# Top-k attention and a squared-ReLU feed: blocks of scores handled two at a time

## The chip, the cores and the metric

The kernel runs on one core of a Trainium2 chip. Its metric is device time in microseconds: the median of three runs was 1082.91 us (1082.89 to 1084.41). Engines have in-order instruction streams of their own: TensorE (PE, with its weight loads shown as PEld), VectorE (DVE), ScalarE (ACT), GpSimd (POOL) and SyncE (SP, which issues all DMAs here). They meet only at semaphores.

## The reference

For 8 batches x 8 heads, q, k and v are 576 x 64 in fp32. The attention keeps, in each row of scores, those not below the row's 32nd largest:

```python
scores = scale * np.matmul(q, k.transpose(0, 1, 3, 2))        # 576 x 576 per head
kth = np.partition(scores, -32, axis=-1)[..., -32:-31]
scores = np.where(scores >= kth, scores, -1e9)
attn = softmax(scores)                                         # exp, sum + 1e-9
x = (attn @ v).transpose(0, 2, 1, 3).reshape(4608, 512)
out = np.maximum(x @ w_in, 0) ** 2 @ w_out                     # 512 -> 2048 -> 512
```

## The kernel before

**Blocks.** A block is 128 query rows by 576 keys. Two heads form a pair (`hp`; 4 pairs in a batch, 32 in all). Queries 0 to 511 of a pair give 4 groups `gi` of two blocks, one for each head; the last 64 queries of both heads share one more block, which goes with `gi` 3. So a pair has 9 blocks, the kernel 288.

**`load_pair`.** SP loads q, k and v of a pair; TensorE transposes q and k into `qk` (head dim on partitions), and GpSimd casts v into `vb` with a column of ones, whose product gives the softmax sums. The last 64 keys of both heads share one 128-row slab of `vb`, kept apart by two multiplications with `heads`.

**`top_k`.** TensorE makes a block's scores with queries on partitions (`scores`, `scores_last`), two halves of 288 keys in two PSUM banks; ScalarE copies them to `s`. The 32nd largest of 576 is found by folding: VectorE takes `m` = max of the two halves (288), and `pp` = max of the halves of `m` (144). GpSimd, through `whole`, makes the other parts by integer arithmetic on the bits: sums `t` of the halves, less the maximum, give the minima, which it writes into `f` behind 144 candidates of `pp`: `mid` (144 more) and `low` (288 more). VectorE then takes eight maxima at a time (`vec.max`) and replaces them (`match_replace`): once over `pp`, then over 144, 288 and 576 columns; each step adds eight, and the last gives `kth`. ScalarE makes `w` = relu(kth - s), which is 0 where a score is kept.

**`attend`.** It runs once for one or two groups `js` (with the 64-query block, where it belongs to them). TensorE computes the scores again, transposed, keys on partitions (`qkT`, fp32), adds `w` transposed and times a steep negative constant (`masked`, bf16 matmuls against `minus`), and ScalarE takes the exponential (`fE`; the last 64 keys apart, `fT4`). TensorE multiplies by `vb` (`fav`), ScalarE copies to `av`, VectorE takes reciprocals, GpSimd scales, TensorE transposes back, ScalarE copies into `xt`.

**`feed`.** When a chunk of `xt` is complete (576 rows; in the last batch 320, 128, 128), two bf16 matmuls with the squared ReLU between follow, and SP stores the rows.

**What sets the order.** Nothing above is emitted in program order. `Plan.op` records each operation with an engine, an assumed duration `dur`, a priority and its dependences; `Plan.schedule` simulates the five engines as a list scheduler and fixes the order of each engine's stream and all buffer slots (`Pool`); `Emitter` turns dependences into semaphore waits. Chip timing differs from the simulated one, but each engine keeps the planned order. Priorities are due times: `PER` us for one block, starting at `T0`. The planner treats VectorE and GpSimd as independent. A second plan with a slower method stands behind a branch and runs only if `verdict` finds ties that break the folding; it doesn't run with these inputs. All matmuls carry line 360 (helper `mm`), all transposes 363 (`tr`), GpSimd's integer operations 514 (`whole`).

Of the kernel before, what the change touches and what calls it, by code (L numbers as in the profile page):

```python
# [12 lines left out]
P = 128  # L13
# [7 lines left out]
class Pool:  # L21
# [16 lines left out]
    def find(self, width):  # L38
        if width == 1:
            if not self.free:  # L40
                return None
            if self.name == "psum":
                half = [s for s in self.free if (s ^ 1) not in self.free]
                s = half[0] if half else self.free[0]
            else:
                s = self.free[0]
            self.free.remove(s)
            return s
        for s in self.free:
            if s % width == 0 and all(s + i in self.free for i in range(width)):  # L50
# [26 lines left out]
class Op:  # L77
    __slots__ = ("eng", "dur", "prio", "fn", "deps", "tiles", "takes", "n", "users", "start", "end",
                 "idx", "sem", "val", "ndma", "seq", "vc", "waits", "wars", "later", "nbf")
# [5 lines left out]
class Plan:  # L85
# [3 lines left out]
    def op(self, eng, dur, prio, fn, r=(), w=(), u=(), hold=(), take=(), after=(), order=(), sem=None, ndma=0, nbf=0.0):  # L89
# [3 lines left out]
        o.eng, o.dur, o.prio, o.fn = eng, dur, prio, fn  # L93
        o.sem, o.ndma, o.seq, o.nbf = sem, ndma, len(self.ops), nbf
# [22 lines left out]
    def schedule(self, t0=0.0, latency=0.12, own=0.07):  # L117
# [22 lines left out]
        done = 0  # L140
        while events:
# [19 lines left out]
            for e in ENGS:  # L161
                if busy[e] > t + 1e-9:
                    continue
                skipped = []
                while ready[e]:
# [22 lines left out]
                    o.start = t  # L188
                    hold = o.dur if e != "sp" else 0.6 * o.ndma
                    o.end = t + o.dur + (hold if e == "sp" else 0)  # L190
                    busy[e] = t + hold
# [85 lines left out]
def bass_top_k_attn__then__act_relu_squared_kernel(  # L277
# [20 lines left out]
    def sb(name, shape, dt=FP32, n=None):  # L298
# [9 lines left out]
    kth = sb("kth", [P, 3, 4 * NPAIR + 8])  # L308
    c16 = sb("c16", [P, 3, 4 * NPAIR + 8])
    c24 = sb("c24", [P, 3, 4 * NPAIR + 8])  # L310
# [7 lines left out]

    sizes = {
        "rq": ([P, 5, 2, D], FP32, 2), "rk": ([P, 5, 2, D], FP32, 2), "rv": ([P, 9, D], FP32, 2),  # L320
        "qk": ([P, 2, S], FP32, 5), "vb": ([P, 10, D + 1], BF16, 5),
        "s": ([P, S], FP32, 8), "m": ([P, HALF], FP32, 4), "pp": ([P, QUART], FP32, 4),
        "t1": ([P, HALF], FP32, 2), "t2": ([P, QUART], FP32, 2), "f": ([P, S], FP32, 4),
        "a": ([P, 3, 8], FP32, 3), "sh": ([P, 3], FP32, 2), "w": ([P, S], BF16, 13),
        "p": ([P, 4, 2, 320], BF16, 3), "p4": ([P, 320], BF16, 3), "av": ([P, 5, D + 1], FP32, 2),
        "x": ([P, 5, D], BF16, 2), "xt": ([P, NCT, S], BF16, 3), "g": ([P, S], BF16, 16),
# [21 lines left out]

    def batch_order(b):
        if b < NB - 1:  # L350
            return ([(hp, g) for hp in range(NHP) for g in range(4)], {1: ([0, 1], False), 3: ([2, 3], True)},
                    [(0, S)])
        return ([(hp, g) for g in (2, 3, 0, 1) for hp in range(NHP)],
                {3: ([2, 3], True), 0: ([0], False), 1: ([1], False)}, [(256, 320), (0, 128), (128, 128)])

    PER = 3.2
    T0 = 12.0

# [3 lines left out]
    def tr(o, i, ident):  # L362
        return pe.matmul(o, i, ident, is_transpose=True, skip_group_check=True)  # L363

    def build(full, weights, pl):
        state = {"n": 0, "u": 0, "g": 0, "z": 0, "last": {}}
# [6 lines left out]
        def load_pair(b, hp, base):  # L373
# [12 lines left out]
            def loadv():  # L386
# [3 lines left out]
                res += [nc.sync.dma_start(r[64 * h:64 * h + 64, 8, :], v[b, 2 * hp + h, 512:576, :])  # L390
                        for h in range(2)]
# [4 lines left out]
            pl.op("sp", 2.3, base - 70, loadv, w=[rv], take=[rv], sem=slot_sem, ndma=4)  # L396
# [22 lines left out]
            pl.op("gp", .62, base + 5, lambda: gp.tensor_copy(at(vb)[:, 0:8, 0:D], at(rv)[:, 0:8, :]),  # L419
                  r=[rv], w=[vb], take=[vb])  # L420
            for h in range(2):
                pl.op("gp", .45, base + 5.1, lambda h=h: gp.tensor_scalar(
                    at(vb)[:, 8 + h, 0:D], at(rv)[:, 8, :], heads[:, h:h + 1], None, ALU.mult), r=[rv], w=[vb])
            return qk, vb

        def top_k(gi, qk, tg, dw):

            nb = 3 if gi == 3 else 2
            n0 = state["n"]
            state["n"] += nb  # L430
            ss = [Tile(psum, 2) for _ in range(nb)]
            st = [tile("s") for _ in range(nb)]

            def scores():
                x = at(qk)
                for half in range(2):
                    ks = HALF * half
                    for h in range(2):
                        ins = mm(bank(ss[h], half)[:, 0:HALF],
                                 x[64 * h:64 * h + 64, 0, 128 * gi:128 * gi + 128],  # L440
                                 x[64 * h:64 * h + 64, 1, ks:ks + HALF], True)
                return ins

            def scores_last():
                x = at(qk)
                for half in range(2):
                    for h in range(2):
                        ha = half ^ h
                        ins = mm(bank(ss[2], ha)[64 * h:64 * h + 64, 0:HALF],
                                 x[64 * h:64 * h + 64, 0, 512:576],  # L450
                                 x[64 * h:64 * h + 64, 1, HALF * ha:HALF * ha + HALF], True)
                return ins

            pl.op("pe", 1.2, tg - 30, scores, r=[qk], w=ss[:2], take=ss[:2] + st[:2])
            if nb == 3:
                pl.op("pe", 1.2, tg - 29, scores_last, r=[qk], w=[ss[2]], take=[ss[2], st[2]])
            for i in range(nb):
                pl.op("act", .64, tg - 28 + i, lambda i=i: act.copy(  # L458
                    at(st[i])[:, :].rearrange("p (a c) -> p a c", a=2),
                    ps32[:, ss[i].slot:ss[i].slot + 2, 0:HALF]), r=[ss[i]], w=[st[i]])  # L460

            a = tile("a")
            dk = [0]
            ix = [state["g"], state["g"], state["z"]]
            state["g"] += 1
            state["z"] += nb == 3

            def dve(dur, fn, **kw):
                dk[0] += 1
                return pl.op("dve", dur, tg + .34 * dk[0], fn, **kw)  # L470

            def eighth(t, i):

                return t[:, i, ix[i] + 7:(ix[i] - 1 if ix[i] else None):-1]
# [6 lines left out]
            ks = []  # L481
            if full:
                f = [tile("f") for _ in range(nb)]
                sh = tile("sh")
                prev = [[] for _ in range(nb)]
                for rnd in range(4):
                    src = st if rnd == 0 else f
                    for i in range(nb):
                        get = dict(r=[st[i]]) if rnd == 0 else dict(hold=[f[i]])
                        if rnd == 3:  # L490
                            ks.append(chain(kth, i, prev[i], .665, lambda i=i: vec.max(
                                eighth(kth, i), at(f[i])[:, :]), **get))
                            continue
                        prev[i] = [dve(.665, lambda i=i, src=src: vec.max(at(a)[:, i, :], at(src[i])[:, :]),
                                       after=prev[i], take=[a, sh] if rnd == 0 and i == 0 else [],
                                       w=[a] if rnd == 0 else [], **(
                                           get if rnd == 0 else dict(hold=[f[i], a])))]
                    if rnd == 3:
                        break
                    if rnd == 0:  # L500
                        prev[nb - 1].append(dve(.08, lambda: vec.tensor_scalar(
                            at(sh)[:, 0:nb], at(a)[:, 0:nb, 0], 0.0, None, ALU.max), r=[a], w=[sh]))
                        prev = [prev[nb - 1] + prev[i] for i in range(nb)]
                    for i in range(nb):
                        prev[i] = [dve(.725, lambda i=i, src=src: vec.match_replace(
                            at(f[i])[:, :], at(a)[:, i, :], at(src[i])[:, :], NEG), after=prev[i],
                            **(dict(r=[st[i]], w=[f[i]], hold=[a], take=[f[i]]) if rnd == 0
                               else dict(hold=[f[i], a])))]
            else:

                m, pp, t1, t2, f = ([tile(nm) for _ in range(nb)] for nm in ("m", "pp", "t1", "t2", "f"))

                def whole(dur, prio, i, op, o, x, y, **kw):
                    return pl.op("gp", dur, prio + .8 * i, lambda: gp.tensor_tensor(  # L514
                        o().bitcast(I32), x().bitcast(I32), y().bitcast(I32), op), **kw)

                low, mid = [], []
                for i in range(nb):
                    A, B = (lambda i=i: at(st[i])[:, 0:HALF]), (lambda i=i: at(st[i])[:, HALF:S])
                    M, L = (lambda i=i: at(m[i])[:, :]), (lambda i=i: at(t1[i])[:, :])  # L520
# [3 lines left out]
                for i in range(nb):  # L524
# [392 lines left out]
```

## Time and profile before

| | |
|---|---|
| median of 3 runs | 1082.91 us |
| profiled execution, its own time | 1080.87 us |
| its span | 1079.0 us |
| busy: DVE / PE / POOL / ACT | 980.8 / 918.1 / 906.7 / 765.9 us |
| mean granted TensorE clock | 0.954 of full speed |
| DMA, mean | 44 GB/s |

The span reaches from the first to the last instruction of one execution. A busy time is the time in which at least one instruction of that engine (or group) runs, so records that overlap by their ends count once. The mean of one record includes its wait inside the engine, and a matmul's record its modelled end; the distance from one start to the next is what an instruction costs in a stream. In a list of instructions in order of time, "x2" merges neighbours of one kind. "Idle before" is what an engine stood still ahead of a group, with the releaser behind the arrow.

### The profile page before, as it was taken

The page shows a single profiled execution, that of the slowest core. Times are in us where ns is not written, and L with a number is a line of the kernel's source. Part 1 is how long each engine was busy: PE and PEld are TensorE (multiplying, and loading weights), DVE is VectorE, ACT ScalarE, POOL GpSimd, SP SyncE. Part 2 cuts the span into 40 slices and gives each one's busy share as a digit, 9 for nine tenths or more (in the row PEclk, how much of TensorE's full clock was granted, in tenths as well). Part 3 has the DMA queues.
Part 4 walks back from the last instruction along what each step waited for, and adds up shares of the span by engine and source line. Part 5 has one row for each costly group of instructions (what it writes and reads, how often), then busy time and mean ns, then how long its engine had stood idle before and what let it go on. Part 6 is the DMA issues. An engine that isn't in the chain of part 4 may idle for free.

```text
span 1079.0 us, 23727 instructions
## 1 busy us (share of the span) xinstructions
PE 918.1 (85%) x8035; PEld 548.5 (51%) x8082; DVE 980.8 (91%) x3538; ACT 765.9 (71%) x1341; POOL 906.7 (84%) x1391
## 2 busy tenths in 40 slices
PE   6766868788899998889888899898888998979897
PEld 4434435444555555545455445555455554644554
DVE  5999999599999999599999999799998899999951
ACT  5645658766698678867688777887688776656652
POOL 7998989689988898588897999789897799999871
PEclk9878789999999999999899999999999999898999
DMA  6533310220200112112110013001220100000001
GB/s 146 130 101 100 111 46 13 56 54 21 71 12 12 53 48 57 23 42 54 28 45 2 24 51 93 23 2 52 67 50 1 44 21 16 2 1 21 21 16 38
DMA packets 124419, 47.77 MB, mean 44 GB/s; under 512 B 116608, under 2 KB 116608, under 8 KB 124288
## 3 DMA queue, kind: packets, MB, share of 16 engines
q1 hardware_dynamic: 124288, 46.16, 16.6%
q8 instruction: 65, 1.06, 0.4%
q14 instruction: 66, 0.54, 0.2%
HBM read 36.70 MB, written 9.44 MB: 43 GB/s over the span
## 4 chain that ended last, share of the span: by engine, by line
DVE 59%; POOL 13%; PE 12%; issue 10%; ACT 5%; SPq 0%; DMA 0%; POOLq 0%; DVEq 0%
DVE kth L553 15%; PE ps L360 12%; DVE c L547 11%; DVE m L522 10%; DVE f L550 8%; POOL f L514 7%; DVE pp L528 7%; POOL t L514 5%; DVE f L541 4%; DVE a L539 3%; ACT w L561 2%; ACT s L458 1%; POOL x L663 1%; PE ps L363 1%; DVE rzall L661 1%
## 5 line engine op out<-in xcount | busy, mean ns | idle before, releaser
L360 PE MATMUL ps<-qk 64*128 64x288 f32 (+7 forms) x2640 | 434.4, 443 | 60.7 <-ACT w L561 19.3
L561 ACT ACTIVATE w<-s,kth 128x576 bf16<-128x576 f32 x288 | 214.5, 771 | 137.3 <-DVE kth L553 136.9
L360 PEld LDWEIGHTS ps<-qk 64*128 64x128 f32 (+1 forms) x2640 | 216.4, 185 | 178.6 <-ACT w L561 33.3
L514 POOL TENSOR_TENSOR t<-s 128x288 int32<-128x288 int32 x288 | 234.0, 823 | 33.0 <-ACT s L458 30.5
L514 POOL TENSOR_TENSOR f<-t,m 128x288 int32<-128x288 int32 x288 | 228.1, 807 | 0.0
L514 POOL TENSOR_TENSOR t<-m 128x144 int32<-128x144 int32 x288 | 180.8, 638 | 49.9 <-DVE m L522 47.8
L550 DVE MATCH_REPLACE8 f<-c,f 128x144 f32<-128x144 f32 (+1 forms) x576 | 206.4, 363 | 0.0
L553 DVE MAX8 kth<-f 128x8 f32<-128x576 f32 x288 | 202.9, 742 | 2.6 <-POOL f L514 2.6
L620 ACT ACTIVATE p<-ps 128x640 bf16<-128x640 f32 (+1 forms) x192 | 155.2, 809 | 57.3 <-PE ps L360 56.0
L522 DVE TENSOR_TENSOR m<-s 128x288 f32<-128x288 f32 x288 | 158.8, 583 | 40.8 <-ACT s L458 40.8
L458 ACT COPY s<-ps 128x576 f32<-128x576 f32 x288 | 170.8, 642 | 33.2 <-PE ps L360 32.6
L547 DVE MAX8 c<-f 128x8 f32<-128x144 f32 (+1 forms) x576 | 190.8, 367 | 2.0 <-POOL f L514 1.9
L360 PE MATMUL ps<-wo,g 128*128 128x512 bf16 (+1 forms) x593 | 151.5, 383 | 8.7 <-ACT p L620 2.1
L360 PE MATMUL ps<-xt,win 128*128 128x288 bf16 (+2 forms) x1088 | 142.9, 284 | 7.4 <-ACT g L706 2.4
L514 POOL TENSOR_TENSOR f<-t,pp 128x144 int32<-128x144 int32 x288 | 141.7, 509 | 3.2 <-DVE pp L528 3.2
L360 PEld LDWEIGHTS ps<-steep_bf,w 128*128 128x128 bf16 (+1 forms) x1600 | 83.6, 102 | 110.4 <-issue 109.4
L528 DVE TENSOR_TENSOR pp<-m 128x144 f32<-128x144 f32 x288 | 131.5, 492 | 0.4
L360 PE MATMUL ps<-steep_bf,w 128*128 128x128 bf16 (+3 forms) x1600 | 124.0, 222 | 0.0
L360 PEld LDWEIGHTS ps<-xt,win 128*128 128x128 bf16 x1088 | 97.4, 99 | 40.0 <-ACT g L704 3.3
L360 PEld LDWEIGHTS ps<-wo,g 128*128 128x128 bf16 (+1 forms) x640 | 56.1, 101 | 60.7 <-issue 8.2
L541 DVE MATCH_REPLACE8 f<-a,pp 128x144 f32<-128x144 f32 x288 | 81.4, 287 | 0.0
L663 POOL TENSOR_TENSOR x<-av,rzall 128x256 bf16<-128x256 f32 (+2 forms) x68 | 43.7, 643 | 44.6 <-DVE rzall L661 43.9
(54 smaller groups left out, 807.7 us busy)
## 6 DMA issues: line engine op xcount, KB each, us to landing
rq<-in_q_dram SPq DMA_DIRECT2D x64, 128.0 KB, 2.4
rk<-in_k_dram SPq DMA_DIRECT2D x64, 128.0 KB, 2.5
rv<-in_v_dram SPq DMA_DIRECT2D x64, 128.0 KB, 2.3
out_dram<-o SPq DMA_DIRECT2D x32, 256.0 KB, 2.1
ws<-in_moe_w_in_dram SPq DMA_DIRECT2D x8, 512.0 KB, 4.4
ws<-in_moe_w_out_dram SPq DMA_DIRECT2D x8, 512.0 KB, 3.6
rq<-in_q_dram SPq DMA_DIRECT2D x32, 32.0 KB, 2.5
rk<-in_k_dram SPq DMA_DIRECT2D x32, 32.0 KB, 2.4
```

The source lines that it names most:

```text
L360: return pe.matmul(o, l, r, start=start, stop=stop, skip_group_check=True)
L458: pl.op("act", .64, tg - 28 + i, lambda i=i: act.copy(at(st[i])[:, :].rearrange("p (a c) -> p a c", a=2), ps32[:, ss[i].slot:ss[i].slot + ...
L514: return pl.op("gp", dur, prio + .8 * i, lambda: gp.tensor_tensor(o().bitcast(I32), x().bitcast(I32), y().bitcast(I32), op), **kw)
L522: dve(.42, lambda i=i, A=A, B=B: vec.tensor_tensor(at(m[i])[:, :], A(), B(), ALU.max), r=[st[i]], w=[m[i]], take=[m[i]])
L528: dve(.27, lambda i=i, M1=M1, M2=M2: vec.tensor_tensor(at(pp[i])[:, :], M1(), M2(), ALU.max), r=[m[i]], w=[pp[i]], take=[pp[i], f[i]] + ([ ...
L541: prev[i] = [dve(.275, lambda i=i: vec.match_replace(at(f[i])[:, 0:QUART], at(a)[:, i, :], at(pp[i])[:, :], NEG), r=[pp[i]], hold=[a], w=[ ...
L547: lambda i=i, t=t, wd=wd: vec.max(eighth(t, i), at(f[i])[:, 0:wd]),
L550: prev[i] = [chain(t, i, prev[i], dur + .06, lambda i=i, t=t, wd=wd: vec.match_replace(at(f[i])[:, 0:wd], eighth(t, i), at(f[i])[:, 0:wd], ...
L553: ks.append(chain(kth, i, prev[i] + [low[i]], .665, lambda i=i: vec.max(eighth(kth, i), at(f[i])[:, :]), hold=[f[i]]))
L561: pl.op("act", .75, tw + .8 * i, lambda i=i: act.activation(at(ws[i])[:, :], at(st[i])[:, :], ACTF.Relu, bias=kth[:, i, ix[i]:ix[i] + 1], ...
L620: return act.activation(o, i, ACTF.Exp, scale=0.125)
L663: pl.op("gp", .15 + .16 * nu, tt + 4, lambda: gp.tensor_tensor(at(xr)[:, 0:nu, :], at(avs)[:, 0:nu, 0:64], rzall[:, u0:u0 + nu].unsqueeze( ...
```

## The change

A group is now two blocks everywhere, kept in one buffer of 2 x 576 columns: 144 groups. The 64-query blocks of two pairs form a group of their own (`Z`), so those groups need two pairs loaded. The folds `m`, `pp` on VectorE and the sums and differences on GpSimd each become one instruction for both blocks; max and match instructions stay one per block. The second block's key columns begin with the last 64 keys, so the two blocks' last 64 keys lie side by side and nine 128-column slices cover a group. `attend` now works on one group: nine fp32 transposes of `s` (`flip`) replace the recomputed scores, the mask matmuls add onto them, and one exponential takes 1152 columns from three PSUM banks. v's last 64 rows are loaded into zeroed slabs (one more DMA per pair), the two multiplications by `heads` go, and all loads of q, k and v wait for those memsets. The planner gets a mark `lk` for the two folds: such an operation starts when GpSimd is idle, and GpSimd is held until it ends. ScalarE's assumed durations drop by 0.05; `PER` is 6.2 for a group, and scores are due `LEAD` = 20 us ahead.

```diff
 # Plan.schedule
-                if busy[e] > t + 1e-9:
+                if busy[e] > t + 1e-9 or (e == "gp" and locked > t + 1e-9):
                     continue
...
-                    o.start = t
+                    o.start = max(t, busy["gp"]) if o.lk else t
                     hold = o.dur if e != "sp" else 0.6 * o.ndma
...
+                    if o.lk:
+                        locked = o.end
 # buffers
-        "s": ([P, S], FP32, 8), "m": ([P, HALF], FP32, 4), "pp": ([P, QUART], FP32, 4),
-        "t1": ([P, HALF], FP32, 2), "t2": ([P, QUART], FP32, 2), "f": ([P, S], FP32, 4),
+        "s": ([P, 2, S], FP32, 6), "m": ([P, 2, HALF], FP32, 3), "pp": ([P, 2, QUART], FP32, 3),
+        "t1": ([P, 2, HALF], FP32, 2), "t2": ([P, 2, QUART], FP32, 2), "f": ([P, 2, S], FP32, 3),
 # top_k: scores of the second block in the order 512:576, 0:512
+            COLS = [[[(0, 288)], [(288, 576)]], [[(512, 576), (0, 224)], [(224, 512)]]]
 # top_k: folds
-                    whole(.81, tg - 1, i, ALU.add, L, A, B, r=[st[i]], w=[t1[i]], take=[t1[i]])
-                    dve(.42, lambda i=i, A=A, B=B: vec.tensor_tensor(at(m[i])[:, :], A(), B(), ALU.max),
-                        r=[st[i]], w=[m[i]], take=[m[i]])
...
+                dve(.67, lambda: vec.tensor_tensor(
+                    at(m)[:, :, :], at(st)[:, :, 0:HALF], at(st)[:, :, HALF:S], ALU.max), lk=True,
+                    r=[st], w=[m], take=[m])
+                whole(1.5, tg - 1, ALU.add, lambda: at(t1)[:, :, :], lambda: at(st)[:, :, 0:HALF],
+                      lambda: at(st)[:, :, HALF:S], r=[st], w=[t1], take=[t1])
+                dve(.37, lambda: vec.tensor_tensor(
+                    at(pp)[:, :, :], at(m)[:, :, 0:QUART], at(m)[:, :, QUART:HALF], ALU.max),
+                    r=[m], w=[pp], take=[pp, f, a], lk=True)
+                whole(.82, tg - .5, ALU.add, lambda: at(t2)[:, :, :], lambda: at(m)[:, :, 0:QUART],
+                      lambda: at(m)[:, :, QUART:HALF], r=[m], w=[t2], take=[t2])
+                mid = whole(.82, tg + .5, ALU.subtract, ...)
+                low = whole(1.5, tg + 2, ALU.subtract, ...)
 # attend
+            def flip(cols, i0):
...
+                for o, c, start in outs:
+                    tr(o, sf[:, c:c + 128], ident32[:, :], start=start, stop=True)
+                for o, c, start in outs:
+                    ins = mm(o, wf[:, c:c + 128], minus[:, :], False)
+            o_t = pl.op("pe", .85, tt, lambda: flip([0, 128, 256, 384], 0), r=[st, wt], w=[e], take=[e, pt])
+            pl.op("pe", 1.05, tt + .1, lambda: flip([640, 768, 896, 1024, 512], 4), r=[st, wt], w=[e], order=[o_t])
+            pl.op("act", 1.15, tt + 1, lambda: act.activation(
+                at(pt)[:, :, :].rearrange("p k q -> p (k q)"),
+                ps32[...][:, 512 * e.slot:512 * e.slot + 1152], ACTF.Exp, scale=0.125), r=[e], w=[pt])
 # setup and main
+        zeros = [pl.op("gp", .3, -97.5, lambda t=t: gp.memset(t[:, 8:12, :], 0.0)) for t in mem["rv"]]
+        if o.eng == "sp":
+            o.deps.update(zeros)
```

## Rows read from the trace of the kernel before

**Rows 1.** The page, part 1: busy us (share of the span) xinstructions.
```profile
PE 918.1 (85%) x8035; PEld 548.5 (51%) x8082; DVE 980.8 (91%) x3538; ACT 765.9 (71%) x1341; POOL 906.7 (84%) x1391
```

**Rows 2.** Two stretches: length; busy (xinstructions) of PE, PEld, DVE, ACT, POOL; PEclk, DMA, GB/s.
```profile
60.00:120.00 60.00, 39.30 (x304) 22.44 (x304) 59.80 (x203) 31.93 (x55) 57.08 (x82) 0.74 0.31 93
240.00:360.00 120.00, 105.45 (x951) 63.52 (x957) 117.09 (x438) 93.73 (x164) 104.70 (x160) 0.99 0.12 31
```

**Rows 3.** The page, part 4: the chain that ended last, by engine.
```profile
DVE 59%; POOL 13%; PE 12%; issue 10%; ACT 5%; SPq 0%; DMA 0%; POOLq 0%; DVEq 0%
```

**Rows 4.** VectorE's waits: who waited for whom, us in total, times, longest.
```profile
DVE m L522 <- ACT s L458: 40.8, 10, 13.4
...
DVE kth L553 <- POOL f L514: 2.6, 1, 2.6
```

**Rows 5.** VectorE in order of time: start us, us, instruction.
```profile
298.58 0.80 DVE L522 TENSOR_TENSOR m<-s 128x288 f32<-128x288 f32 x2
299.30 0.73 DVE L528 TENSOR_TENSOR pp<-m 128x144 f32<-128x144 f32 x3
299.96 0.72 DVE L539 MAX8 a<-pp 128x8 f32<-128x144 f32 x3
```

**Rows 6.** VectorE's folds, grouped: busy us, mean ns | idle before.
```profile
L522 DVE TENSOR_TENSOR m<-s 128x288 f32<-128x288 f32 x288 | 158.8, 583 | 40.8 <-ACT s L458 40.8
L528 DVE TENSOR_TENSOR pp<-m 128x144 f32<-128x144 f32 x288 | 131.5, 492 | 0.4
```

**Rows 7.** All engines in order of time, about a `pp` that met a sum.
```profile
320.96 1.07 POOL L514 TENSOR_TENSOR t<-s 128x288 int32<-128x288 int32 x1 [3.08 <-ACT s L458]
...
321.41 0.79 DVE L528 TENSOR_TENSOR pp<-m 128x144 f32<-128x144 f32 x1
322.00 0.55 POOL L514 TENSOR_TENSOR t<-m 128x144 int32<-128x144 int32 x1
```

**Rows 8.** GpSimd in order of time, beside the stretch of rows 5.
```profile
299.09 1.29 POOL L514 TENSOR_TENSOR t<-m 128x144 int32<-128x144 int32 x1 [1.13 <-DVE m L522]
```

**Rows 9.** GpSimd's integer line: duration ns min/median/max, first and last start.
```profile
L514 POOL TENSOR_TENSOR t<-s x288: 782/793/1086, 11.1 to 1039.7; 128x288 int32<-128x288 int32 x144
L514 POOL TENSOR_TENSOR t<-m x288: 478/552/1662, 12.1 to 1040.5; 128x144 int32<-128x144 int32 x144
L514 POOL TENSOR_TENSOR f<-t,pp x288: 477/487/962, 14.1 to 1044.4; 128x144 int32<-128x144 int32 x144
```

**Rows 10.** The same line over the whole span: length, busy POOL (x), PEclk, DMA, GB/s.
```profile
0.00:1079.00 1079.00, 764.83 (x1152) 0.95 0.17 44
```

**Rows 11.** TensorE's matmuls, grouped (the first holds all forms of score matmuls).
```profile
L360 PE MATMUL ps<-qk 64*128 64x288 f32 (+7 forms) x2640 | 434.4, 443 | 60.7 <-ACT w L561 19.3 <-ACT xt L680 12.4 <-ACT p L620 11.2
L360 PE MATMUL ps<-qk 64*128 64x288 f32 x1024 | 170.8, 455 | 18.8 <-ACT xt L680 12.4 <-ACT s L458 4.0 <-ACT p L620 1.3
L360 PE MATMUL ps<-qk 64*64 64x288 f32 x256 | 38.0, 415 | 1.4 <-ACT p L620 0.9 <-ACT s L458 0.5
L363 PE MATMUL ps<-ident,rq 128*128 128x128 f32 x128 | 21.5, 292 | 7.7 <-DMA rq<-in_q_dram 6.4 <-ACT s L458 1.3
```

**Rows 12.** ScalarE's large exponentials, grouped by form.
```profile
L620 ACT ACTIVATE p<-ps 128x640 bf16<-128x640 f32 x128 | 90.1, 704 | 29.9 <-PE ps L360 28.7
L620 ACT ACTIVATE p<-ps 128x1024 bf16<-128x1024 f32 x64 | 65.2, 1018 | 27.5 <-PE ps L360 27.3
```

**Rows 13.** The start, in order of time.
```profile
0.73 1.00 SPq L379 DMA_DIRECT2D rq<-in_q_dram  x2
...
10.40 1.18 ACT L458 COPY s<-ps 128x576 f32<-128x576 f32 x2 [2.39 <-PE ps L360]
11.07 0.46 DVE L522 TENSOR_TENSOR m<-s 128x288 f32<-128x288 f32 x1 [11.07 <-ACT s L458]
```

**Rows 14.** VectorE in order of time, its last `kth`.
```profile
1046.03 1.51 DVE L553 MAX8 kth<-f 128x8 f32<-128x576 f32 x2
```

**Rows 15.** The core: span and mean granted clock.
```profile
core 0: 1079.0 us, clock 0.954
```

More of the change, by code (lines that the diff above doesn't have):

```diff
@@ L48, in find @@
             return s
-        for s in self.free:
-            if s % width == 0 and all(s + i in self.free for i in range(width)):
+        for s in sorted(self.free):
+            if (width == 3 or s % width == 0) and all(s + i in self.free for i in range(width)):
                 for i in range(width):
@@ L463, in top_k @@
+            pl.op("pe", 1.2 if gi != Z else 2.4, tg - LEAD, scores if gi != Z else scores_z,
+                  r=sorted(set(qks), key=lambda t: t.num), w=ss, take=ss + [st])
+            cp = []
+            for i in range(2):
+                cp.append(pl.op("act", .65, tg - LEAD + 2 + i, lambda i=i: act.copy(
+                    at(st)[:, i, :].rearrange("p (a c) -> p a c", a=2),
+                    ps32[:, ss[i].slot:ss[i].slot + 2, 0:HALF]), r=[ss[i]], w=[st]))
             dk = [0]
-            ix = [state["g"], state["g"], state["z"]]
@@ L500, in top_k @@
                     if rnd == 0:
[L501 to L504, printed above, removed]
+                        prev[1].append(dve(.08, lambda: vec.tensor_scalar(
+                            at(sh)[:, :], at(a)[:, :, 0], 0.0, None, ALU.max), r=[a], w=[sh], take=[sh]))
@@ new lines, in top_k @@
+                mid = whole(.82, tg + .5, ALU.subtract, lambda: at(f)[:, :, QUART:HALF], lambda: at(t2)[:, :, :],
+                            lambda: at(pp)[:, :, :], r=[t2, pp], w=[f])
+                low = whole(1.5, tg + 2, ALU.subtract, lambda: at(f)[:, :, HALF:S], lambda: at(t1)[:, :, :],
+                            lambda: at(m)[:, :, :], r=[t1, m], w=[f])
+                for i in range(2):
+                    prev[i] = [dve(.215, lambda i=i: vec.max(at(a)[:, i, :], at(pp)[:, i, :]), r=[pp], w=[a])]
@@ new lines, in top_k @@
+                for i in range(2):
+                    prev[i] = [dve(.275, lambda i=i: vec.match_replace(
+                        at(f)[:, i, 0:QUART], at(a)[:, i, :], at(pp)[:, i, :], NEG),
+                        r=[pp], hold=[a], w=[f], after=prev[i])]
+                for t, wd, dur, more in ((c16, QUART, .215, []), (c24, HALF, .365, [mid])):
+                    for i in range(2):
+                        prev[i] = [chain(t, i, prev[i] + more, dur, lambda i=i, t=t, wd=wd: vec.max(
+                            eighth(t, i), at(f)[:, i, 0:wd]), hold=[f])]
+                    for i in range(2):
@@ L550, in top_k @@
                         prev[i] = [chain(t, i, prev[i], dur + .06, lambda i=i, t=t, wd=wd: vec.match_replace(
-                            at(f[i])[:, 0:wd], eighth(t, i), at(f[i])[:, 0:wd], NEG), hold=[f[i]])]
-                for i in range(nb):
-                    ks.append(chain(kth, i, prev[i] + [low[i]], .665, lambda i=i: vec.max(
-                        eighth(kth, i), at(f[i])[:, :]), hold=[f[i]]))
+                            at(f)[:, i, 0:wd], eighth(t, i), at(f)[:, i, 0:wd], NEG), hold=[f])]
@@ L555, in top_k @@
+                for i in range(2):
+                    ks.append(chain(kth, i, prev[i] + [low], .665, lambda i=i: vec.max(
+                        eighth(kth, i), at(f)[:, i, :]), hold=[f]))
             kths.extend(ks)
-            tw = tg + PER * nb + dw
-            ws = [tile("w") for _ in range(nb)]
+            tw = tg + PER
+            wt = tile("w")
             if not full:
-                for i in range(nb):
-                    pl.op("act", .75, tw + .8 * i, lambda i=i: act.activation(
-                        at(ws[i])[:, :], at(st[i])[:, :], ACTF.Relu, bias=kth[:, i, ix[i]:ix[i] + 1], scale=-1.0),
-                        r=[st[i]], w=[ws[i]], take=[ws[i]], after=[ks[i]])
-                return ws
@@ L566, in top_k @@
[L566 to L569 removed]
+                for i in range(2):
+                    pl.op("act", .77, tw + .8 * i, lambda i=i: act.activation(
+                        at(wt)[:, i, :], at(st)[:, i, :], ACTF.Relu, bias=kth[:, i, n:n + 1], scale=-1.0),
+                        r=[st], w=[wt], take=[wt] if i == 0 else [], after=[ks[i]])
@@ L570, in top_k @@
+                return st, wt
+            for i in range(2):
+                o = pl.op("gp", .75, tw + 1.3 * i, lambda i=i: gp.tensor_scalar(
+                    at(f)[:, i, :], at(st)[:, i, :], kth[:, i, n:n + 1], STEEP, ALU.subtract, ALU.mult),
+                    r=[st], hold=[f], after=[ks[i]])
                 pl.op("gp", .75, tw + 1.3 * i + .65, lambda i=i: gp.tensor_scalar(
-                    at(ws[i])[:, :], at(st[i])[:, :], BIG, at(sh)[:, i:i + 1], ALU.min, ALU.max),
-                    r=[st[i], sh], w=[ws[i]], take=[ws[i]])
@@ L836, in bass_top_k_attn__then__act_relu_squared_kernel @@
     main = Plan()
-    early, pre, weights = setup(main)
+    early, pre, zeros, weights = setup(main)
     n_pre = len(main.ops)
```

363 lines of the change are left out of this document (148 added, 215 removed).

## The prediction

> **What bounds the kernel now.** I read the busy times first [rows 1]: VectorE 91%, TensorE 85%, GpSimd 84%, ScalarE 71%. A share of the whole span hides stages, so the stretches come next [rows 2]: from 240 to 360 us VectorE is busy 117.1 of 120 us, GpSimd 104.7, TensorE 105.5. The chain that ended last [rows 3] is 59% VectorE, 13% GpSimd. Apart from its start VectorE waits little: 40.8 us for scores in SBUF, 11 of them the start, and 2.6 us once for GpSimd's last subtraction [rows 4]. So VectorE's own sequence sets the pace, and the question is what its instructions cost.
>
> Its max and match instructions take the same time everywhere; its folds don't. A 288-wide fold `m` begins 0.36 us after the one before it, and a 144-wide `pp` 0.22 us, where nothing disturbs them: 299.30 - 298.58 over two, 299.96 - 299.30 over three; their records are 0.44 and 0.29 us [rows 5]. Over all 288 blocks the means are 583 and 492 ns [rows 6]. The excess, 143 and 202 ns, times 288 is 41 + 58 = 99 us, 0.69 us for two blocks. Its cause is seen in one place [rows 7]: GpSimd's sum `t` begins, VectorE's `pp` is issued while it runs, takes 0.79 us in place of 0.29, and GpSimd's next sum starts about when `pp` ends. It works in the other direction too [rows 8]: a 144-wide sum that takes 478 ns at its shortest [rows 9] takes 1.29 us while five folds pass. A fold of VectorE and an instruction of GpSimd exclude each other, each for its whole length.
>
> **Folds, the step on the path.** Removed: 576 folds. Added: 288 pair-wide ones. Columns cost (0.36 - 0.22)/144 = 0.97 ns each, so 576 take 0.64 us and 288 take 0.36. A group pays 1.00 us where two blocks pay 2 x 0.58 = 1.16: 0.16 x 144 groups = 23 us saved. The max and match instructions stay one for each block.
>
> **The wait at the folds.** All 99 us of it go, and another one comes, because GpSimd's instructions get longer. They go from 793 (288 wide) and 487 ns (144 wide) [rows 9] by 2.1 ns a column to about 1.41 us (576 wide, extrapolated) and 0.79. A group needs 2 x 1.41 + 2 x 0.79 = 4.40 us of GpSimd in place of 5.12. A fold that comes at a random moment into that work meets, on average, a rest of (2 x 1.41^2 + 2 x 0.79^2)/(2 x 4.40) = 0.59 us; by the same sum it is 0.34 us today, so 0.69 us for two blocks are about two full waits among four folds. Bounds: 0, if GpSimd stands still when a fold comes; 2 x 0.59 = 1.19 us a group, if both folds meet it (2 x 1.41 = 2.8 if both always come at a start, which no row suggests). I take one wait a group: today five folds in a row went through undisturbed while GpSimd's next sum depended on the first of them [rows 5, 8], and the planner now starts a fold where it has GpSimd idle and holds GpSimd until it ends, so the second fold follows the first. GpSimd's other work is 906.7 - 764.8 = 142 us today [rows 1, 10], some 120 with one cast in place of three instructions at `vb`: 4.40 + 0.83 = 5.2 us of the 5.9 us of a 6.9 us period that are not fold. One wait is 0.59 x 5.2/5.9 = 0.52 us, times 144 = 75 us.
>
> **Behind that step.** VectorE then waits for `low`, GpSimd's widest subtraction. After `m` ends come `t2`, `mid` and `low`, 0.79 + 0.79 + 1.41 = 2.99 us plus hand-overs of some 0.1 us each; VectorE reaches `kth` after `pp` and six pairs of instructions, near 4.0 us. Cover of 0.7 us, cost nothing; if GpSimd slips one sum of 1.41 us in between, `kth` is 0.7 us late (a rival below). Freed GpSimd time is not on the path.
>
> **TensorE.** Recomputed transposed scores go: 434.4 - 170.8 - 38.0 = 225.6 us of matmul records [rows 11]; the mask matmuls get fewer, 9 for each of 144 groups. Added are 1296 fp32 transposes; those of q took 21.5/128 = 0.168 us each, 218 us. Splitting one score matmul of the second block in two adds one for each group. Net within +-30 us of 918: it stays under VectorE (105.5 of 120 against 117.1). If VectorE speeds up by 4%, TensorE stands near 91%, and its cover is thin.
>
> **ScalarE.** 144 exponentials of 1152 columns at 1.018 + 128 x 0.314/384 = 1.12 us [rows 12] are 162 us, for 90.1 + 65.2 = 155.3 us and the small exponentials of the last 64 keys, which go; the copies of `av` become smaller and more. At 71% busy this hides behind VectorE. The exponential needs all nine transposes, in three PSUM banks of eight rather than two; later weights cost nothing while the six `s` pairs keep the scores ahead. Bounds: -30 us (the waits for scores behind the start vanish, [rows 4]) to +30 (they double); I take 0.
>
> **Loads and start.** `v` needs five DMAs for four: the DMA engines are 12% busy in the steady stretch [rows 2], nothing. All input loads now wait for two memsets of `rv` on GpSimd; the first load is issued at 0.73 us [rows 13]. Two memsets of at most some 0.3 us behind the identity's put it about 1 us later, all of it on the path to the first fold; bounds 0.5 and 2. The first fold also needs both score copies (1.18 us for two, from 10.40; it starts today at 11.07 [rows 13], after one): 0.6 us. Together 2 us. Behind the last `kth`, which ends near 1047.5 [rows 14], 31 us remain for attention of the last blocks, the last feed and its store; equal in both.
>
> **Sum.** The profiled execution took 1080.87 us (span 1079.0), 0.2% under the median of the timed runs. 1080.9 - 23 - 99 + 75 + 2 = 1036 us.
>
> **Rivals.**
> (a) *GpSimd is idle when folds come.* It has less work, and an order that waits for `pp` keeps it from running ahead. Wait 0.15 us a group, 22 us: 983. Against it: 5.2 us of 5.9 is nearly full.
> (b) *The wait grows: slower.* Place: `m` and `pp` of a group are apart, or a sum of 1.41 us that needs only the scores is queued at the gap between them, as in [rows 7], where the sum got in first. Two waits of 0.59: 171 us, so 1080.9 - 23 - 99 + 171 + 2 = 1132. It decides from (23 + 99 - 2)/144 = 0.83 us a group. For it: half the folds wait today; against it: [rows 5]. The Trainium skill's page "SBUF — State Buffer" (section "SBUF: two separate sides") says the same of the mechanism, that the side which starts first holds the shared ports for its whole instruction and the other blocks fully; read alone it speaks against making GpSimd's instructions longer. The trace agrees on the holding (0.79 us for 0.29); no row has a longer holder of this kind.
> (c) *The wait moves to `kth` or `c24`.* GpSimd takes the next group's sum before `low`: 0.7 us late in a quarter to half of the groups, 25 to 50 us: 1060 to 1085. Against it: 2.6 us in total today.
> (d) *TensorE's clock falls.* Its granted clock was 0.99 from 240 to 360 us, with TensorE 88% busy, and 0.74, a mixture of the two levels of 1.2 and 2.4 GHz, from 60 to 120 us, with it 65% busy [rows 2]. If transposes held the clock up less than the matmuls they replace, and it averaged 0.80 in place of 0.954 [rows 15], some 905 us of work would become 905 x 0.954/0.80 = 1079, with start and end about 1114: slower. The Trainium skill, "TensorE: Matmul & The Clock Gate" (section "Part 4: PE-mode transpose"), says that transposes don't count as activity for the full clock. No row here has transposes alone. Against it: scores, masks, value products and the feed stay between them.
>
> **How the numbers follow.** Forecast 0.51 (its own range 1005 to 1062); (a) 0.22; (b) 0.10; (c) 0.10; (d) 0.07. Time 1036; from 970 (below it would need no waits and fewer idle gaps, 0.07) to 1090 (above lie most of (b) and (d), 0.12). A difference under 0.2%, 2 us, can't be told from none. Faster: 0.51 + 0.22 + 0.07 of (c) = 0.80; within 0.2%: 0.03; slower: 0.17.
>
> **What would show it.** Right: `m` near 0.7 to 0.9 us and `pp` 0.45 to 0.75 in the mean, together about 0.5 us over their undisturbed length; GpSimd's wide sums near 1.41 us, its busy time near 780; TensorE near 900 us at a clock over 0.93; `kth` waiting for `low` under 15 us. Wrong: folds 0.83 us or more a group above undisturbed (b), or none (a); waits at `kth` and `c24` of 25 us (c); a clock under 0.85 in the steady stretch with VectorE waiting for scores (d); a first fold later than 14 us.

## The result, and the profile after

The changed kernel takes 1044.91 us (median of 4; 1042.58 to 1046.28), against 1082.97 for the one before: a ratio of 0.9643, 95% interval 0.9623 to 0.9663. The forecast was 1036, and 1005 to 1062 for the likeliest case. The profiled execution took 1045.51 us with a span of 1043.7.

The page's busy times, then the chain that ended last by engine, of the changed kernel:

```profile
PE 878.8 (84%) x8034; PEld 645.3 (62%) x8034; DVE 938.9 (90%) x3268; ACT 756.7 (73%) x1321; POOL 815.7 (78%) x778
...
DVE 51%; PE 21%; ACT 17%; POOL 5%; issue 3%; DMA 1%; SPq 1%; POOLq 0%; DVEq 0%
```

The span fell by 35.3 us against [rows 1]: VectorE's busy time by 41.9, while its idle time rose from 98.2 to 104.8. VectorE still leads the chain, but less than in [rows 3]. The folds, grouped (busy, mean ns | idle before), answer to [rows 6]:

```profile
L532 DVE TENSOR_TENSOR m<-s 128x576 f32<-128x576 f32 x144 | 140.5, 987 | 34.1 <-ACT s L477 33.4 <-POOL f L529 0.7
L537 DVE TENSOR_TENSOR pp<-m 128x288 f32<-128x288 f32 x144 | 101.0, 711 | 0.7
```

158.8 + 131.5 us have become 140.5 + 101.0. VectorE's busy time as a whole fell by less, 41.9, since fewer records also mean fewer overlaps of their ends. Undisturbed, VectorE in order of time shows records of 0.75 and 0.44 us, and `m` and `pp` back to back at 0.67 and 0.37 us, as against [rows 5]:

```profile
301.38 0.44 DVE L537 TENSOR_TENSOR pp<-m 128x288 f32<-128x288 f32 x1
301.75 0.75 DVE L532 TENSOR_TENSOR m<-s 128x576 f32<-128x576 f32 x1
302.42 0.30 DVE L547 MAX8 a<-pp 128x8 f32<-128x144 f32 x1
```

So the waits inside the folds are (987 - 750 + 711 - 440) ns x 144 = 73 us, for 99 before. One of the long ones, all engines, as in [rows 7]:

```profile
319.80 0.76 DVE L532 TENSOR_TENSOR m<-s 128x576 f32<-128x576 f32 x1 [7.11 <-ACT s L477]
...
319.84 1.97 POOL L529 TENSOR_TENSOR t<-s 128x576 int32<-128x576 int32 x1 [9.90 <-ACT s L477]
...
320.59 1.54 DVE L537 TENSOR_TENSOR pp<-m 128x288 f32<-128x288 f32 x1
```

GpSimd's sum is issued 0.04 us into `m`, runs when `m` is done, and `pp` lies behind it: 1.54 us in place of 0.44. GpSimd's integer groups answer to [rows 9]; their means hold such waits, the undisturbed 576-wide one takes 1.41 us (the median):

```profile
L529 POOL TENSOR_TENSOR t<-s 128x576 int32<-128x576 int32 x144 | 210.8, 1467 | 24.6 <-ACT s L477 24.6
L529 POOL TENSOR_TENSOR f<-t,m 128x576 int32<-128x576 int32 x144 | 211.1, 1466 | 0.0
L529 POOL TENSOR_TENSOR f<-t,pp 128x288 int32<-128x288 int32 x144 | 141.4, 982 | 40.7 <-DVE pp L537 40.4
L529 POOL TENSOR_TENSOR t<-m 128x288 int32<-128x288 int32 x144 | 139.4, 968 | 22.2 <-DVE m L532 22.2
```

VectorE's waits on others, against [rows 4] (who for whom, us, times, longest):

```profile
DVE rzall L628 <- ACT av L620: 42.3, 24, 5.5
DVE m L532 <- ACT s L477: 33.4, 9, 15.3
DVE c L554 <- POOL f L529: 11.6, 8, 6.6
```

The first of them in the kernel before, which [rows 4] leave out:

```profile
DVE rzall L661 <- ACT av L659: 28.9, 12, 7.9
```

15.3 us of the scores' wait are the start, in order of time, against [rows 13]:

```profile
0.74 0.87 SPq L788 DMA_DIRECT2D ws<-in_moe_w_in_dram  x2
0.88 0.32 POOL L771 MEMSET rv<- 128x256 f32 x1
...
1.46 0.31 POOL L771 MEMSET rv<- 128x256 f32 x1
...
1.80 0.97 SPq L394 DMA_DIRECT2D rq<-in_q_dram  x2
...
8.23 1.11 PE L378 MATMUL ps<-ident,rq 128*128 128x128 f32 x4 [8.23 <-DMA rq<-in_q_dram]
...
15.25 0.76 DVE L532 TENSOR_TENSOR m<-s 128x576 f32<-128x576 f32 x1 [15.25 <-ACT s L477]
```

The two memsets hold q's load to 1.80 us. But SP's order now begins with two weight loads, which wait for nothing, and q reaches TensorE at 8.23 us. TensorE's and ScalarE's new groups follow, against [rows 11, 12], and then two stretches (length; busy PE, PEld, DVE, ACT, POOL; PEclk, DMA, GB/s) against [rows 2]:

```profile
L378 PE MATMUL ps<-ident,s 128*128 128x128 f32 x1296 | 214.6, 297 | 88.4 <-ACT w L568 65.9
L602 ACT ACTIVATE p<-ps 128x1152 bf16<-128x1152 f32 x144 | 161.6, 1129 | 93.0 <-PE ps L375 92.9
```

```profile
60.00:120.00 60.00, 39.98 (x344) 32.47 (x344) 59.57 (x195) 34.09 (x58) 50.09 (x45) 0.80 0.36 98
240.00:360.00 120.00, 107.88 (x987) 78.30 (x985) 111.40 (x394) 93.18 (x163) 95.83 (x89) 0.96 0.17 43
```

### The profile page after: what moved, and what is told of

It is laid out like the page before. It is cut to its first block, busy times and chain, and to the rows that moved or that the text cites. A ratio compares the mean times of both kernels' runs of the same rounds, so it can differ in the third digit from the quotient of the medians.

```text
span 1043.7 us, 22267 instructions
## 1 busy us (share of the span) xinstructions
PE 878.8 (84%) x8034; PEld 645.3 (62%) x8034; DVE 938.9 (90%) x3268; ACT 756.7 (73%) x1321; POOL 815.7 (78%) x778
## 4 chain that ended last, share of the span: by engine, by line
DVE 51%; PE 21%; ACT 17%; POOL 5%; issue 3%; DMA 1%; SPq 1%; POOLq 0%; DVEq 0%
PE ps L375 14%; DVE kth L560 10%; DVE f L557 10%; DVE c L554 9%; DVE m L532 8%; PE ps L378 7%; ACT w L568 6%; DVE pp L537 5%; DVE f L549 5%; ACT s L477 4%; DVE a L547 4%; ACT p L602 2%; POOL f L529 2%; ACT g L680 1%; ACT g L696 1%
## 5 line engine op out<-in xcount | busy, mean ns | idle before, releaser
L378 PE MATMUL ps<-ident,s 128*128 128x128 f32 x1296 | 214.6, 297 | 88.4 <-ACT w L568 65.9
L375 PE MATMUL ps<-qk 64*128 64x288 f32 (+4 forms) x1600 | 221.8, 402 | 15.5 <-ACT p L602 6.3
L529 POOL TENSOR_TENSOR t<-s 128x576 int32<-128x576 int32 x144 | 210.8, 1467 | 24.6 <-ACT s L477 24.6
L602 ACT ACTIVATE p<-ps 128x1152 bf16<-128x1152 f32 x144 | 161.6, 1129 | 93.0 <-PE ps L375 92.9
L378 PEld LDWEIGHTS ps<-ident,s 128*128 128x128 f32 x1296 | 152.3, 151 | 121.5 <-ACT w L568 72.7
L529 POOL TENSOR_TENSOR f<-t,m 128x576 int32<-128x576 int32 x144 | 211.1, 1466 | 0.0
L554 DVE MAX8 c<-f 128x8 f32<-128x144 f32 (+1 forms) x576 | 188.6, 368 | 11.6 <-POOL f L529 11.6
L529 POOL TENSOR_TENSOR f<-t,pp 128x288 int32<-128x288 int32 x144 | 141.4, 982 | 40.7 <-DVE pp L537 40.4
L532 DVE TENSOR_TENSOR m<-s 128x576 f32<-128x576 f32 x144 | 140.5, 987 | 34.1 <-ACT s L477 33.4
L529 POOL TENSOR_TENSOR t<-m 128x288 int32<-128x288 int32 x144 | 139.4, 968 | 22.2 <-DVE m L532 22.2
L375 PE MATMUL ps<-steep_bf,w 128*128 128x128 bf16 x1296 | 130.0, 232 | 0.0
L537 DVE TENSOR_TENSOR pp<-m 128x288 f32<-128x288 f32 x144 | 101.0, 711 | 0.7
```

Source lines behind the costliest of these rows:

```text
L375: return pe.matmul(o, l, r, start=start, stop=stop, skip_group_check=True)
L529: return pl.op("gp", dur, prio, lambda: gp.tensor_tensor(o().bitcast(I32), x().bitcast(I32), y().bitcast(I32), op), **kw)
L532: dve(.67, lambda: vec.tensor_tensor(at(m)[:, :, :], at(st)[:, :, 0:HALF], at(st)[:, :, HALF:S], ALU.max), lk=True, r=[st], w=[m], take=[m])
L537: dve(.37, lambda: vec.tensor_tensor(at(pp)[:, :, :], at(m)[:, :, 0:QUART], at(m)[:, :, QUART:HALF], ALU.max), r=[m], w=[pp], take=[pp, f, ...
L554: prev[i] = [chain(t, i, prev[i] + more, dur, lambda i=i, t=t, wd=wd: vec.max(eighth(t, i), at(f)[:, i, 0:wd]), hold=[f])]
L602: pl.op("act", 1.15, tt + 1, lambda: act.activation(at(pt)[:, :, :].rearrange("p k q -> p (k q)"), ps32[:, :, :].rearrange("p b c -> p (b ...
```

## The experiments

Each is built on the changed kernel unless it says otherwise. Ratios are to the kernel before, run beside it. "Fold waits" are worked out as above, from the grouped means less 750 and 440 ns (440 and 290 for block-wide folds), times the count.

### GpSimd's folds cut to a few columns (x_tiny)

```diff
-    o().bitcast(I32), x().bitcast(I32), y().bitcast(I32), op), **kw)
+    o().bitcast(I32)[:, :, 0:8], x().bitcast(I32)[:, :, 0:8], y().bitcast(I32)[:, :, 0:8], op), **kw)
+        for t in mem["f"]:
+            pl.op("dve", 1.2, -94, lambda t=t: vec.memset(t[:, :, :], -1.0e30))
```

> GpSimd's four integer instructions of a group work on the first 8 columns of each block only, in the order planned before; the minima are left out of the search (the rest of f holds one constant). Theory (a fold and a GpSimd instruction exclude each other for their whole length, and VectorE's sequence sets the pace): m falls from 987 to about 760 ns and pp from 711 to about 450, 73 us together, and the 12 us at c24 go too: 945 to 975 us. Rival (TensorE and ScalarE are as near to the limit as VectorE): the folds get short, but VectorE waits as much more for scores and for av, and the time stays above 1000.

The minima are left out of the search here. 995.4 us (one run): more than the theory's 945 to 975, less than the rival's 1000. Its folds:

```profile
L532 DVE TENSOR_TENSOR m<-s 128x576 f32<-128x576 f32 x144 | 111.1, 782 | 32.3 <-ACT s L477 32.2
L537 DVE TENSOR_TENSOR pp<-m 128x288 f32<-128x288 f32 x144 | 66.2, 470 | 0.7
```

Waits of 9 us are left of 73, so GpSimd's long instructions are what lengthened the folds. The time fell by 50 only: VectorE's idle time rose from 104.8 to 115.9 us, with 62.5 (for 42.3) at the reciprocals' wait for `av`. Theory and rival each hold in part: in this planned order, the next limit begins behind some 50 us of fold waits.

### Block-wide folds on VectorE again (x_narrow)

```diff
-                dve(.67, lambda: vec.tensor_tensor(
-                    at(m)[:, :, :], at(st)[:, :, 0:HALF], at(st)[:, :, HALF:S], ALU.max), lk=True,
+                dve(.67, lambda: [vec.tensor_tensor(
+                    at(m)[:, i, :], at(st)[:, i, 0:HALF], at(st)[:, i, HALF:S], ALU.max) for i in range(2)][-1], lk=True,
```

(the same for `pp`)

> VectorE's two pair-wide folds are issued as two block-wide ones each, same plan, same GpSimd instructions. Theory: the fixed part of an instruction comes back, (2 x 0.36 + 2 x 0.22) - (0.67 + 0.36) = 0.13 us a group, 19 us, and GpSimd's next instruction gets in between the halves in some groups, 0.1 to 0.3 us more: 1065 to 1105. Rival (the width of the folds is worth nothing, the gain came from the plan and TensorE): 1040 to 1050.

1115.71 us, ratio 1.0291 (1.0258 to 1.0324): slower than the kernel before.

```profile
L532 DVE TENSOR_TENSOR m<-s 128x288 f32<-128x288 f32 x288 | 190.6, 706 | 30.4 <-ACT s L477 30.0 <-POOL f L529 0.4
L537 DVE TENSOR_TENSOR pp<-m 128x144 f32<-128x144 f32 x288 | 131.7, 501 | 0.7
```

Fold waits of 266 and 211 ns x 288 = 137 us, nearly twice 73; I had expected 14 to 43 us of that increase of 64, and 1105 us at most. VectorE's busy time rose by 79.6 us (938.9 to 1018.5), the fixed part and the waits together; the time rose by 71. Each fold instruction meets GpSimd for itself: counted over the trace, 179 of 576 folds are longer than the shortest of their kind by over 0.1 us, by 0.77 us in the mean; in the changed kernel 113 of 288 are, by 0.67. With GpSimd's long instructions, the pair-wide folds on VectorE are worth all of the gain and more.

### Block-wide instructions on GpSimd again (x_split)

```diff
-                    return pl.op("gp", dur, prio, lambda: gp.tensor_tensor(
-                        o().bitcast(I32), x().bitcast(I32), y().bitcast(I32), op), **kw)
+                    return pl.op("gp", dur, prio, lambda: [gp.tensor_tensor(
+                        o().bitcast(I32)[:, i, :], x().bitcast(I32)[:, i, :], y().bitcast(I32)[:, i, :], op)
+                        for i in range(2)][-1], **kw)
```

> Each of GpSimd's pair-wide integer instructions is issued as two block-wide ones, same plan, VectorE's folds stay pair-wide. Theory (a fold waits for the rest of the one instruction that runs): a wait that is met shrinks from 0.68 to about 0.37 us, 73 us of fold waits become about 40, while GpSimd gets some 100 us more work, which costs up to 20 us at c24 and kth: 1010 to 1040. Rival (what counts is how many GpSimd instructions there are, or its share of time): fold waits of 73 us or more, and 1050 to 1080.

1047.91 us, 0.9665 (0.9646 to 0.9685).

```profile
L533 DVE TENSOR_TENSOR m<-s 128x576 f32<-128x576 f32 x144 | 133.4, 937 | 36.0 <-ACT s L477 34.0 <-POOL f L529 2.0
L538 DVE TENSOR_TENSOR pp<-m 128x288 f32<-128x288 f32 x144 | 102.2, 720 | 0.7
```

Fold waits of 67 us: the total hardly moved, against the theory. Counted in the same way, 174 of 288 folds are now lengthened, by 0.41 us in the mean, for 113 by 0.67. The single wait shrinks with the instruction that it meets, but GpSimd, busy for 904 us in place of 816, is met more often, and the waits at `c24` rose from 11.6 to 21.5 us. The width on GpSimd's side is worth nothing that shows at the folds.

### Without the planner's mark (x_nolk)

```diff
-    dve(.67, lambda: ..., lk=True, r=[st], w=[m], take=[m])
+    dve(.67, lambda: ..., r=[st], w=[m], take=[m])
```

(the same for `pp`)

> The planner's mark on the folds is taken away, so it plans VectorE and GpSimd as independent; all instructions are the same, their order is not. Theory (the planned order keeps it to one wait a group): the waits at the folds grow from 73 to 100 to 170 us, and the time to 1065 to 1130. Rival (GpSimd's share of time alone decides how often a fold is met): fold waits of 65 to 85 us, time within 10 us of 1045.

1052.50 us, 0.9712 (0.9686 to 0.9738). Means of 895 and 731 ns: fold waits of 63 us, fewer than in the changed kernel. The 7.6 us lost are idle time (117.9 us; the waits for scores went from 33.4 to 54.8). The planned orders with the mark that were run have fold waits of 60 to 73 us, and this one lies among them: the mark does not hold the waits down.

### Early loads, planned anew (x_early) and in the old order (x_start)

```diff
 # x_early
-        if o.eng == "sp":
+        if o.eng == "sp" and o.ndma == 5:
             o.deps.update(zeros)
 # x_start, after main.schedule() of the changed kernel: 5 DMAs are v's loads
+    sp = main.order["sp"]
+    for o in sp:
+        if o.ndma != 5:
+            o.deps.difference_update(zeros)
+    early_ws = [o for o in sp[:2]]
...
+    main.order["sp"] = sp = sp[2:4] + early_ws + sp[4:]
```

> Only v's loads wait for the two memsets, those of q and k don't. Theory (the wait let two weight loads of 512 KB pass ahead of the first q and k, and held those up): the first q load is issued at 0.7 us again, the first fold starts at 11.5 to 12.2 us in place of 15.25, and the time falls by 3 to 5 us, to 1040 to 1042. Rival (the start is hidden later, by what TensorE and ScalarE lag): first fold as early, time within 1.5 us of 1045.

> The plan is made as in the changed kernel; afterwards the first loads of q and k are put ahead of the two weight loads and no longer wait for the memsets. Every other engine's order is the same, instruction for instruction. Theory (the late start alone costs what it shows, the rest of the earlier variant's 30 us came from its other planned order): first fold at 11.5 to 12.2 us, time 1040 to 1043, and the gaps of VectorE from 540 to 690 us stay. Rival (the weights' place at the start holds up the whole run): 1015 to 1025.

x_early took 1015.33 us, 0.9358 (0.9333 to 0.9384), 30 us less than the changed kernel where 3 to 5 were expected, with the first fold at 11.96 us as expected. So its own theory explains a few us of 30, and x_start was made to find the rest: same start (first fold at 11.94), all other engines in the old order.

```profile
0.74 1.00 SPq L394 DMA_DIRECT2D rq<-in_q_dram  x2
...
11.94 0.76 DVE L532 TENSOR_TENSOR m<-s 128x576 f32<-128x576 f32 x1 [11.94 <-ACT s L477]
```

1042.08 us, 0.9602 (0.9565 to 0.9639): 2.8 us for the start, with an interval that overlaps the changed kernel's. The other 27 came with the new planned order: fold waits of 60 us (934 and 676 ns) for 73, and idle time of 86.0 us for 104.8.

### One priority moved by 1 us (x_lead21), and the same in the kernel before (b_due31, b_due29)

```diff
-    LEAD = 20
+    LEAD = 21
 # b_due31, in the kernel before (b_due29: 29, 28 and 27)
-            pl.op("pe", 1.2, tg - 30, scores, ...)
+            pl.op("pe", 1.2, tg - 31, scores, ...)
 # scores_last and the copies to s move alike
```

> One priority is moved by 1 us: scores are due 21 us ahead in place of 20; instructions, sizes and waits are the same, the planned order is another one. Theory (the planned order alone moves the time by tens of microseconds, through VectorE's idle gaps, while folds and their waits stay): undisturbed fold lengths unchanged, fold waits 60 to 80 us, time off 1045 by 5 to 25 us, either way. Rival (resources set the time, order hardly): within 3 us of 1045.

1019.55 us, 0.9402 (0.9368 to 0.9435): 25 us faster with the same instructions.

```profile
DVE rzall L628 <- ACT av L620: 33.8, 23, 5.7
DVE m L532 <- ACT s L477: 25.8, 5, 15.1
```

Fold waits of 63 us (928 and 699 ns), idle time 89.1: some 10 us less in the one and 16 in the other, both from the order. In the trace 62% of VectorE's instructions and 75% of ScalarE's stand at another place in their engine's stream than in the changed kernel (the n-th of a kind is matched with the n-th).

> The kernel before, with its scores due 1 us earlier in the planner's priorities (31 us ahead in place of 30); nothing else. Theory (a planned order is worth tens of microseconds in either kernel): time off 1083 by 5 to 30 us, waits at the folds 85 to 110 us as before, the rest in VectorE's idle time. Rival (only the changed kernel is that touchy, since its buffers are tighter): within 4 us of 1083.

> The same the other way: scores due 29 us ahead. Theory: time off 1083 by 5 to 30 us, either way, fold waits 85 to 110 us. Rival: within 4 us of 1083. If both stay above 1046, the gain of the change is more than a lucky order against an unlucky one.

1085.13 us, 1.0011 (1.0001 to 1.0021), and 1084.31, 1.0008 (0.9998 to 1.0019). The time does not move, but the theory is not tested by that, since the planned order hardly moved either: 1.6% of VectorE's instructions and 4.4% of ScalarE's stand at another place in b_due31, 0.3% and 1.0% in b_due29. What another order would be worth in the kernel before stays open. The planned orders of the changed kernel that were run lie between 1015 and 1053 us; none comes near 1083.

### Reciprocals later (x_rzlate), and with early loads (x_early_rz)

```diff
-            rz = pl.op("dve", .1, tt + 4, ...)
+            rz = pl.op("dve", .1, tt + 10, ...)
 # the product on GpSimd: tt + 10, the transposes behind it: tt + 11
```

> The reciprocals, the product on GpSimd and the transposes behind them get priorities 6 us later, so VectorE's stream has them behind more of its other work. Theory (VectorE stands still at a reciprocal because the planner has it too early, while max and fold instructions are ready behind it): its 42 us of waits for av fall below 20, and the time to 1015 to 1030. Rival (av is late because TensorE and ScalarE are as busy as VectorE, and the wait only changes its name): waits for scores grow by as much, time within 5 us of 1045.

> The early loads (only v's wait for the memsets) and the reciprocals 6 us later, together, planned anew. If their effects add: 1015 - 6 = 1009. If the planned order decides more than either: anywhere from 1005 to 1040, with fold waits of 60 to 75 us and the difference in VectorE's idle time.

1038.39 us, 0.9594 (0.9565 to 0.9623), and 1036.12, 0.9538 (0.9491 to 0.9585). Later priorities took the waits for `av` from 42.3 to 36.0 us only, and those for scores rose from 33.4 to 45.2: nearer to the rival. On top of early loads they cost 21 us in place of gaining 6. The effects of these two edits don't add.

### Five of nine transposes left out (x_lesspe)

```diff
-                for o, c, start in outs:
-                    tr(o, sf[:, c:c + 128], ident32[:, :], start=start, stop=True)
+                if i0 == 0:
+                    for o, c, start in outs:
+                        tr(o, sf[:, c:c + 128], ident32[:, :], start=start, stop=True)
...
-                    ins = mm(o, wf[:, c:c + 128], minus[:, :], False)
+                    ins = mm(o, wf[:, c:c + 128], minus[:, :], start and i0 > 0)
```

> Five of a group's nine transposes are left out (the exponentials of those keys see only the mask); masks, product and plan stay. TensorE's work falls by 720 x 0.17 = 120 us. Theory (TensorE is covered by VectorE, and only adds lateness at av): the waits for av and for scores fall by 10 to 25 us, and the time to 1020 to 1038. Rival (TensorE sets the pace by now): the time falls by more than 35 us, under 1010. Rival (its clock hangs on the transposes): the mean granted clock moves by more than 0.02.

1031.04 us, 0.9525 (0.9497 to 0.9553). The plan is the changed kernel's. TensorE's busy time fell by 59 us, half of what the records promised, the waits for `av` from 42.3 to 30.1 us, the time by 14: TensorE doesn't set the pace, it delays. The granted clock fell to 0.924 from 0.946; with fewer transposes it was lower, not higher, by 0.022, which meets that rival's mark of 0.02. In x_narrow, which has all of them, it was 0.930.

## Why the prediction was right, and where it was not

- **Fixed part of the folds, 23 us.** Mis-sized: 0.67 + 0.37 = 1.04 us back to back for 1.00 forecast, so 0.12 us a group is saved in place of 0.16, 17 us for 23.
- **Waits of 99 us go, 75 come.** The sum is right (73), its reason isn't. I put the one wait a group down to the planner's mark and to adjacency. Without the mark there are 63 us (x_nolk). What holds is the sum's other half: a fold waits for the rest of the instruction that it meets, and the number of fold instructions counts (x_narrow: 137 us for twice as many). It is 113 waits for 288 folds, 0.78 of 0.67 us a group, where the sum had 5.2/5.9 = 0.88 of 0.59 us.
- **Rival (b), two waits a group.** Not met: 73/144 = 0.51 us a group, and it decides from 0.83. That longer instructions on GpSimd are dearer to the folds is refuted as far as x_split goes: half the width, nearly the same waits.
- **Rival (a).** Not met; x_tiny shows that even with nearly no fold waits the time is 995, not 983 or less, since idle time grows.
- **Start, 2 us.** Mis-sized: 4.2 (15.25 less 11.07). The memsets cost 1.07 as said (q's load at 1.80 for 0.73). In x_start, where q and k wait for neither memsets nor weights, the first fold starts at 11.94: 0.87 more than before, for 0.6 forecast for the second score copy. The 2.2 us left came from a step that I had not followed past its queue: once q and k had to wait, SP's order put two weight loads ahead.
- **Behind the step, `low`.** Right in that `kth` never waits; `c24` does, 11.6 us in 8 times, through `mid`. 6.6 us of it are one wait near the end. Rival (c), 25 us or more, is not met.
- **TensorE within 30 us of 918.** 878.8, 39 less and so outside these bounds; the transposes took 214.6 us for 218. It stays under VectorE, but its thin cover, which I had named, got no price; the next point has it.
- **ScalarE, PSUM and TensorE's cover, 0 us.** This step failed, though inside its bounds of 30 us. Between the first fold and the end of the last `kth` VectorE's idle time rose from 60.1 to 71.0 us. I had read that VectorE waits little, and had passed over the reciprocals' 28.9 us for `av`. These became 42.3, while the waits for scores behind the start, on which I had put my bounds, fell from 29.7 (40.8 less 11.07) to 18.1 (33.4 less 15.25). Part of the wait for `av` is TensorE's work: without five of nine transposes it is 30.1 (x_lesspe). The exponential takes 1129 ns (1.12 forecast), but its place is not free. In the longest gap of the middle, VectorE stands still from 312.68 to 319.80 us:

```profile
311.27 1.41 DVE L560 MAX8 kth<-f 128x8 f32<-128x576 f32 x2
...
312.49 1.27 PE L378 MATMUL ps<-ident,s 128*128 128x128 f32 x5
...
314.95 1.14 PE L375 MATMUL ps<-xt,win 128*128 128x288 bf16 x8
315.01 2.13 ACT L602 ACTIVATE p<-ps 128x1152 bf16<-128x1152 f32 x2
...
317.19 1.36 PE L375 MATMUL ps<-qk 64*128 64x288 f32 x10 [0.53 <-ACT p L602]
...
318.58 1.18 ACT L477 COPY s<-ps 128x576 f32<-128x576 f32 x2
```

 Two groups' exponentials run one behind the other, and the next score matmuls start 0.05 us after the second. Score matmuls read nothing that an exponential writes, so what they wait for there is its banks, three of eight for each. But TensorE stands still for them 0.53 us only. For the rest of the gap it works: on two groups' transposes and masks, on the feed and on a value product, which its order has ahead of these scores. Over the whole run its score matmuls wait 6.3 us for exponentials:

```profile
L375 PE MATMUL ps<-qk 64*128 64x288 f32 (+4 forms) x1600 | 221.8, 402 | 15.5 <-ACT p L602 6.3
```

 So the exponentials' banks are a small part of this gap. What makes the order count so much is not shown; no run gave the exponential other banks.
- **The end.** Not equal: 23.3 us behind the last `kth` (1020.4 to 1043.7) for 31.5 before [rows 14]. These 8 us, for which I had given no reason, make up for most of the 11 us by which the idle time ahead of them grew.
- **Rival (d), the clock.** 0.946 for 0.954 [rows 15], 0.96 for 0.99 from 240 to 360 us, and 0.80 for 0.74 from 60 to 120 [rows 2]. Not met. The Trainium skill ("TensorE: Matmul & The Clock Gate", section "Part 4: PE-mode transpose") says that transposes don't count as activity for the full clock. x_lesspe does not agree: with 720 of them left out the clock fell to 0.924. But x_narrow's 0.930 is nearly as low with none left out, so what lowered it stays open.
- **The sum, -45 us.** By the spans it is -35.3: VectorE's busy time -41.9 for -23 - 99 + 75 = -47, the start 4.2 for 2, idle time between the first fold and the last `kth` 10.9 for 0, behind it -8.4 for 0. That 1045 came so near to 1036 is in part luck: two of these errors offset each other, and planned orders of the same instructions differ by up to 37 us.

The version to keep is x_early: 1015.33 us, 6.4% under the kernel before and 2.8% under the changed one, most of it by a luckier order.

## What to carry to other kernels

Where two engines exclude each other, count the instructions of the one that sets the pace: half as many folds meant little more than half the time in waits (73 us for 137), while the length of the other engine's instructions moved their size and their number against each other. A planner that orders everything from assumed durations can be worth nearly as much as the change under test (27 of x_early's 30 us beside 38); move one priority by a trifle, look in the trace whether the order moved, and time both versions before a few per cent are put down to an edit. And when loads get a new condition, look at what passes them in their queue.

## What was not expected of the hardware

A fold that meets GpSimd waits for one instruction, not for the queue behind it: in 110 of the 113 waits counted in the changed kernel exactly one GpSimd instruction ended, and in the other three a second one had ended within the fold's first 0.05 us. So it was in x_split too, where a second half stood right behind (173 of 174; in the one other, of 2.50 us, three sums ended). fp32 transposes of 128 x 128 took 0.166 us each in the stream (214.6/1296).
